# One expert-mixture kernel, four edits: state decay on GpSimd, rows turned in three stages, first expert's W2 split ahead of its gate, first expert's rows scaled by ScalarE

## The chip, the cores and the metric

The kernel runs on one core of one Trainium2 chip. The metric is the device time of one execution in microseconds, the median of several. The engines are named as in the profile: PE is TensorE, PEld its weight loads, DVE is VectorE, ACT is ScalarE, POOL is GpSimd, SP is SyncE, which here only issues transfers.

## The reference

A linear attention with a decay for each head, in blocks, feeds a mixture of eight experts of which each token takes two.

```python
for b in range(nb):                      # q, k, v: 4 x 8 x 768 x 64, blocks of 64
    intra = einsum('bhic,bhjc->bhij', qb, kb) * Dmask[None]
    intra = einsum('bhij,bhjd->bhid', intra, vb)
    inter = einsum('bhid,bhde->bhie', qb * lam_pow[None], kv_state)
    out[:, :, sl] = intra + inter
    kv_state = lam_block * kv_state + einsum('bhsd,bhse->bhde', kb * rev_pow[None], vb)
x = out as 3072 x 512
noisy_logits = x @ w_gate + log1p(exp(x @ w_noise)) * noise
top2, top2_w = the two largest of 8 and their softmax
for e in range(8):                       # w1: 512 x 1024, w2: 1024 x 512
    out[mask] += top2_w[mask] * (relu(x[mask] @ w1[e]) @ w2[e])
```

## The kernel before

The instructions of every engine are issued in the order in which the program text emits them; nothing is reordered. Each engine works through its own queue, and an instruction that waits holds up everything behind it on that engine. There is therefore no planner of costs, only a hand-written order and a small one for the routing: `jobs` is a list of generators (the gate, the routing, the building of key blocks), and `advance(n)` emits steps of them on DVE until an amount of estimated time is used up. Where an `advance` stands decides where in DVE's queue those steps lie.

**Attention.** Twelve steps `u`, each of two chunks `a` of 128 tokens of one batch; three steps make a batch. A step turns K and Q on PE (`trans_k` L344, `trans_q` L360), forms the state's increment (`kv` L435, from `KD`, which POOL scales in `kdecay`, L376), the products inside the chunk (`scores` L388, masked by DVE at L391; `intra`, L400) and the products with the state (`inter`, L400, which read the decayed queries `qTs` and the states `SA`). Before, DVE makes `qTs` from PSUM (L367; for step 1 at L724), and `state` (L439) makes the next state by four multiply-adds for each chunk (L447), or a copy where a batch begins (L444). `KD` has one buffer, so `kdecay` of the next step waits until PE has read the last one in `kv`. `logits`, `gate`, `weights` and `route` (L498 to L640) choose experts for a third of the tokens at a time; their work tiles lie in one tile called `arena`. `pool_keys` (L659) and `keys` (L648) build one-hot blocks, on POOL and on DVE, from which PE makes the lists of rows (`enlist`, L684).

**Experts.** Weights and rows are split into two half-precision parts each (hi by ACT, lo by DVE), and every product is made of three matmuls. For every expert a first product (`gemm1`, L995, eight groups `f` of twelve matmuls for each of two or three parts of its tiles) is followed by a second (`gemm2`, L1040, or L1051 for a short last tile, over tiles of 128 tokens). `evac1` (L1001 on ACT, L1005 on DVE) takes every group out of PSUM: ACT writes hi, then DVE writes the rest lo. `pS` has four banks.

From the third expert on, rows are gathered in pieces and turned by DVE itself: `turn_rows` transposes a tile (L935) and ACT then copies it to half precision (L937) in the same call; `split_rows` makes lo (L947) and gives the buffers to the next gathers. Four tiles are turned during the `gemm2` of the expert before, the others while the first part of `gemm1` runs, at `f` even; `parts` puts the later tiles first, so that the part of four tiles comes second, and its first group needs the last turned tile.

**The first expert** (e = 0) has three parts, of two, two and three tiles, since its rows are gathered while routing still goes on. In part 0 the gate of the last third of the tokens is advanced on DVE between the `split_w(2, 0, j)` of W2 and the evacuations. In `half_lists`, called inside `gemm2` of tile 0, DVE reads the second lists (L699) and POOL gathers two tiles (L919), which `trans_rows` (L974 on PE, L976 on ACT, L977 on DVE) turns inside `gemm2` of tile 1. Results go to `PV` (L1046 on DVE) and are scattered by POOL.

Of the kernel before, what the change touches and what calls it, by code (L numbers as in the profile page):

```python
# [31 lines left out]
C = 128  # L32
# [101 lines left out]
def kernel(  # L134
# [215 lines left out]
    def trans_q(u, banks=()):  # L350

        scaled = not banks
        banks = iter(banks)
        qT[u] = aw.tile([128, HP, 2 * C], FT, name="qT", bufs=1)
        qTs[u] = aw.tile([128, HP, 2 * C], FT, name="qTs")
        for a in range(2):
            nm = next(banks, None)
            p = psum.tile([128, HP, C], FT, name=nm) if nm else bank()
            for hp in range(HP):
                nc.tensor.transpose(p[:, hp, :], QT[u][:, a, 2 * hp:2 * hp + 2, :], identf)  # L360
            cs = slice(a * C, (a + 1) * C)
            if u:
                nc.scalar.activation(qT[u][:, :, cs], p, AF.Copy)
            else:
                nc.vector.tensor_copy(qT[u][:, :, cs], p)
            if scaled and (u % NW or a):
                nc.vector.tensor_mul(qTs[u][:, :, cs], p, QS)  # L367
# [71 lines left out]
    def state(u):  # L439

        for a, p in enumerate(KV[u]):
            sn = SA[u + a, 1 - a] = next(states)
            if (u, a) not in SA:
                nc.vector.tensor_copy(sn, p[:, :, :D])  # L444
                continue
            for hp in range(HP):
                nc.vector.scalar_tensor_tensor(sn[:, hp, :], SA[u, a][:, hp, :], QS[:, hp, C - 1:C], p[:, hp, :D],  # L447
                                               op0=MULT, op1=ADD)
# [272 lines left out]
    state(0)  # L721
# [13 lines left out]
    state(1)  # L735
# [38 lines left out]
    WR = [rp.tile([128, NT], FT, name=f"wr{i}") for i in range(2)]  # L774
    W8 = [rp.tile([128, NT, E - 1], FT, name=f"w8{i}") for i in range(2)]
# [154 lines left out]
    def turn_rows(e, t):  # L930
# [6 lines left out]
        nc.scalar.activation(xt(0, slice(t * TS, t * TS + size(e, t))), raw, AF.Copy, scale=xsc[:, NG - 1:])  # L937
        turned.append((e, t, raw))

    def split_rows():  # L940

        if not turned:
            return
        e, t, raw = turned.pop(0)
# [84 lines left out]
    def gemm2(e, t, then={}):  # L1029
# [6 lines left out]
        if n == TS:  # L1036
# [5 lines left out]
            if e:  # L1042
                nc.vector.scalar_tensor_tensor(o, p, w, pv, op0=MULT, op1=ADD)  # L1043
                scatter_out(e, t, o)
            else:
                nc.vector.tensor_scalar(o, p, w, winv0[:n, part_of(t):part_of(t) + 1], op0=MULT, op1=MULT)  # L1046
# [9 lines left out]
        else:  # L1056
            nc.vector.tensor_scalar(w, w, winv0[:n, part_of(t):part_of(t) + 1], None, op0=MULT)
# [37 lines left out]
    for t in range(NST):  # L1095
# [6 lines left out]
        elif u < NST:  # L1102
            kv(u)
            state(u)
            kdecay(t + 2)
# [4 lines left out]
            trans_q(u)  # L1110
        if t in SQUARES:
# [76 lines left out]
    units = {1: [(1, c, 1, PV[c - 4].bitcast(BF)) for c in range(4, GB[2] - GB[1])], 2: []}  # L1188
    for unit in units[1][:POOLED]:
        pool_keys(*unit)  # L1190
    jobs.extend((build(units[1][POOLED:]), routing(NG - 1), build(units[2])))
    for f in range(2):
        evac1(0, 0, PARTS0[0], f, head[f])
    advance(1.0)
# [21 lines left out]
    def half_lists():  # L1216
        while not built:
            advance(0.01)
# [11 lines left out]
    for i, (t0, n) in enumerate(parts(0)):  # L1230
        for f in range(FB):
# [10 lines left out]
            if i == 0:  # L1242
                if f in (2, 4, 6, 7):
                    split_w(2, 0, (2, 4, 6, 7).index(f))
                else:
                    advance(FILL1)
# [16 lines left out]
        unscale(winv0[:, i:i + 1], 0, None)  # L1263
        if i == 2:
# [87 lines left out]
    for e in range(1, E):  # L1352
# [6 lines left out]
        for i, (t0, n) in enumerate(parts(e)):  # L1359
            for f in range(FB):  # L1360
# [3 lines left out]
                if e > 1 and i == 0 and f % 2 == 0:  # L1364
                    split_rows()
                    if nxt:
                        turn_rows(e, nxt.pop(0))
# [18 lines left out]
        split_rows()  # L1386
        assert not turned
        row_weights(e)
        nxt = tile_order(e + 1) if e + 1 < E else []
        for t in range(tiles(e)):  # L1390
# [3 lines left out]
            if e + 1 < E:  # L1394
# [5 lines left out]
                split_rows()  # L1400
                if t < EARLY:
                    turn_rows(e + 1, nxt.pop(0))
    with tc.For_i(0, n_over) as it:
# [79 lines left out]
```

## Time and profile before

| what | value |
|---|---|
| median of 3 runs | 698.88 us (695.11 to 699.32) |
| the profiled execution | 703.04 us, its span 701.2 us |
| busy PE, DVE, POOL, ACT | 669.4, 414.6, 371.3, 306.3 us |
| mean granted TensorE clock of the span | 0.988 |

The profile is one execution of its own, and its time lies 4.16 us above the median of the runs. The span runs from the first to the last instruction; 1.84 us lie around it. Attention fills the first 146 us, the first expert reaches to 231 us, and the other seven take the rest. Busy time is an average over these; which wait counts is read from the stage.

### The profile page before, as it was taken

The page shows a single profiled execution, that of the slowest core. Times are in us where ns is not written, and L with a number is a line of the kernel's source. Part 1 is how long each engine was busy: PE and PEld are TensorE (multiplying, and loading weights), DVE is VectorE, ACT ScalarE, POOL GpSimd, SP SyncE. Part 2 cuts the span into 40 slices and gives each one's busy share as a digit, 9 for nine tenths or more (in the row PEclk, how much of TensorE's full clock was granted, in tenths as well). Part 3 has the DMA queues.
Part 4 walks back from the last instruction along what each step waited for, and adds up shares of the span by engine and source line. Part 5 has one row for each costly group of instructions (what it writes and reads, how often), then busy time and mean ns, then how long its engine had stood idle before and what let it go on. Part 6 is the DMA issues. An engine that isn't in the chain of part 4 may idle for free.

```text
span 701.2 us, 15983 instructions
## 1 busy us (share of the span) xinstructions
PE 669.4 (95%) x6073; PEld 401.7 (57%) x6073; DVE 414.6 (59%) x1058; ACT 306.3 (44%) x528; POOL 371.3 (53%) x524
## 2 busy tenths in 40 slices
PE   8899899998999999999998999899999999999994
PEld 6788788884765464464445445544554474456441
DVE  4744878988746755664655465556656554565510
ACT  2257567772228453326433633363344436433300
POOL 4512162374154585668767846784677578531221
PEclk9999999999999999999999999999999999999997
DMA  9899888474574562525551545164427434411110
GB/s 200 221 260 235 222 233 229 150 266 156 132 230 150 156 193 84 172 59 157 173 175 43 170 143 174 45 197 131 147 71 210 145 101 145 144 46 39 58 52 33
DMA packets 94193, 104.32 MB, mean 149 GB/s; under 512 B 41235, under 2 KB 66845, under 8 KB 94113
## 3 DMA queue, kind: packets, MB, share of 16 engines
q1 hardware_dynamic: 79456, 65.73, 33.4%
q0 software_dynamic: 13552, 37.00, 16.4%
q8 instruction: 49, 0.80, 0.5%
q10 hardware_dynamic: 1104, 0.53, 0.4%
q14 instruction: 32, 0.25, 0.1%
HBM read 78.28 MB, written 26.12 MB: 149 GB/s over the span
## 4 chain that ended last, share of the span: by engine, by line
PE 66%; DVE 13%; issue 8%; DMA 4%; POOL 4%; ACT 2%; ACTq 0%; POOLq 0%; DVEq 0%
PE pS L995 26%; PE pKV L1040 13%; PE pO L1040 13%; PE pO L400 2%; DVE ht L1005 2%; PE pS L388 2%; PE pS L344 2%; DMA pv<-out_dram,rec 1%; POOL out_dram L1066 1%; DVE at L391 1%; PE pS L435 1%; PE pS L466 1%; PE pS L360 1%; ACT xth L937 1%; POOL xg L908 1%
## 5 line engine op out<-in xcount | busy, mean ns | idle before, releaser
L1040 PEld LDWEIGHTS <-ht 128*128 128x128 f16 x1152 | 112.2, 98 | 135.7 <-issue 3.1
L995 PE MATMUL pS<-xtl,w1h 128*128 128x512 f16 (+3 forms) x544 | 175.8, 323 | 4.7 <-DVE xtl L947 4.7
L995 PE MATMUL pS<-xth,w1h 128*128 128x512 f16 (+3 forms) x544 | 175.7, 323 | 3.7 <-ACT xth L937 2.0
L908 POOL DMA_INDIRECT xg<-x_tok,recq x147 | 153.6, 1045 | 45.9 <-issue 41.0
L995 PE MATMUL pS<-xth,w1l 128*128 128x512 f16 (+3 forms) x544 | 175.7, 323 | 0.0
L995 PEld LDWEIGHTS <-w1h 128*128 128x128 f16 x1088 | 105.5, 98 | 72.3 <-issue 8.0
L1005 DVE SCALAR_TENSOR_TENSOR ht<-pS,ht 128x256 f16<-128x256 f32 (+3 forms) x176 | 75.6, 455 | 103.5 <-ACT ht L1001 102.9
L1001 ACT ACTIVATE ht<-pS 128x512 f16<-128x512 f32 (+3 forms) x136 | 63.1, 479 | 147.6 <-PE pS L995 144.7
L1040 PE MATMUL pKV<-w2h,ht 128*128 128x512 f16 x384 | 119.1, 381 | 0.0
L1040 PE MATMUL pO<-w2h,ht 128*128 128x512 f16 x384 | 118.1, 379 | 0.0
L1066 POOL DMA_INDIRECT out_dram<-ot,rec x46 | 61.5, 1337 | 102.7 <-DVE ot L1043 73.6
L937 ACT ACTIVATE xth<-turned,xsc 128x512 f16<-128x512 f32 (+1 forms) x39 | 27.2, 697 | 120.5 <-DVE turned L935 120.5
L995 PEld LDWEIGHTS <-w1l 128*128 128x128 f16 x544 | 53.3, 98 | 38.7 <-issue 6.1
L1040 PE MATMUL pO<-w2l,ht 128*128 128x512 f16 x192 | 72.8, 379 | 1.1 <-DVE w2l L873 1.1
L1040 PE MATMUL pKV<-w2l,ht 128*128 128x512 f16 x192 | 73.3, 382 | 0.0
L855 ACT ACTIVATE junk<-wst 128x1024 bf16<-128x1024 f32 x64 | 67.0, 1046 | 0.0
L376 POOL TENSOR_TENSOR kd<-kt,Mk 128x512 f32<-128x512 f32 x24 | 24.8, 1051 | 79.0 <-PE pR L435 55.5
L1024 POOL DMA_INDIRECT pv<-out_dram,rec x46 | 52.6, 1144 | 13.4 <-issue 13.4
L873 DVE SCALAR_TENSOR_TENSOR w2l<-wst,wsc,w2h 128x1024 f16<-128x1024 f32 x32 | 41.1, 1284 | 9.1 <-ACT w2h L872 8.6
L1043 DVE SCALAR_TENSOR_TENSOR ot<-pO,wr,pv 128x512 f32<-128x512 f32 x21 | 15.8, 751 | 49.7 <-PE pO L1040 49.1
L391 DVE TENSOR_TENSOR at<-pS,Mk 128x512 f32<-128x512 f32 x48 | 29.9, 682 | 22.9 <-PE pS L388 19.8
L873 DVE SCALAR_TENSOR_TENSOR w1l<-wst,wsc,w1h 128x1024 f16<-128x1024 f32 x32 | 40.6, 1275 | 0.0
(261 smaller groups left out, 896.2 us busy)
## 6 DMA issues: line engine op xcount, KB each, us to landing
wst<-in_moe_w_dram SPq DMA_DIRECT2D x36, 512.0 KB, 3.6
wst<-in_moe_w_dram SPq DMA_DIRECT2D x96, 128.0 KB, 2.8
x_tok<-xc SPq DMA_DIRECT2D x24, 272.0 KB, 5.0
kt<-in_k_dram SPq DMA_DIRECT2D x12, 512.0 KB, 4.5
qt<-in_q_dram SPq DMA_DIRECT2D x24, 256.0 KB, 5.7
vt<-in_v_dram SPq DMA_DIRECT2D x12, 512.0 KB, 6.0
out_dram<-zero SPq DMA_DIRECT2D x24, 256.0 KB, 3.8
xg<-x_tok,recq POOLq DMA_INDIRECT x147, 2.8
```

The costliest lines, as they stand in the source:

```text
L376: nc.gpsimd.tensor_mul(kd[:, :, s], kt[:, :, s], mask(s, slice(0, HP), slice(C - 1, C)).to_broadcast([128, HP, 2, D]))
L391: nc.vector.tensor_mul(at[:, s], ps[s], mask(s, slice(2 * r, 2 * r + 2), slice(0, C)))
L855: nc.scalar.activation(junk, WS[which, e, j], AF.Square, accum_out=wsq[:, which - 1, j:j + 1])
L873: nc.vector.scalar_tensor_tensor(lo[:, r], st[:, r], s, hi[:, r], op0=MULT, op1=SUB)
L908: nc.gpsimd.indirect_dma_start(out=XG[t][:, g * QW:(g + 1) * QW], out_offset=None, in_=x_tok.rearrange("t (q w) -> (t q) w", w=QW), in_off ...
L937: nc.scalar.activation(xt(0, slice(t * TS, t * TS + size(e, t))), raw, AF.Copy, scale=xsc[:, NG - 1:])
L995: nc.tensor.matmul(p, W1[a][d][:, fs], xt(b, cs)[:, d], start=(d == 0 and i == 0), stop=(d == DB - 1 and i == 2))
L1001: nc.scalar.activation(ht(e, 0, f, cs), p, AF.Relu)
L1005: nc.vector.scalar_tensor_tensor(ht(e, 1, f, c), p[:, r], 0.0, ht(e, 0, f, c), op0=OP.max, op1=SUB)
L1024: nc.gpsimd.indirect_dma_start(out=PV[t][:size(e, t), :], out_offset=None, in_=out, in_offset=bass.IndirectOffsetOnAxis(ap=REC[e, t], axis=0),
L1040: nc.tensor.matmul(p, ht(e, a, f, cs), W2[b][f // 2][:, f % 2, :], start=(i == 0), stop=(i == len(terms) - 1))
L1066: st = nc.gpsimd.indirect_dma_start(out=out, out_offset=bass.IndirectOffsetOnAxis(ap=REC[e, t], axis=0), in_=o, in_offset=None, bounds_che ...
```

## The change

Four things change. Nothing of the mathematics does.

1. **Attention.** The decayed queries come from POOL, out of the half of `qT` that ACT has written, not from DVE out of PSUM. The state is made in two parts: POOL multiplies the last state by its decay into a tile `sd` (`decay`), and DVE adds the increment from PSUM in one instruction for each chunk. `decay` of the next chunk is emitted directly behind `state`. In the loop the second chunk's `state` and `kdecay` now stand behind `trans_q`, and the gathers of the first expert stand between the two halves.
2. **Turned rows.** The copy by ACT has a function of its own, `copy_rows`, called one group `f` (or one tile of `gemm2`) after the turn. `split_rows` takes what has been copied.
3. **First expert, part 0.** `advance(1.0)` and the advances at `f` = 3 and 5 go. Only the one key block that DVE builds is emitted at `f` = 3. The gate begins inside `half_lists`. Of the four key blocks of the last third, POOL builds one (`late`), and DVE three.
4. **First expert's output.** ACT copies the sums with the row's weight as scale; the scale of the part is multiplied into the weights once for each part on DVE.

```diff
@@ trans_q, state
-                nc.vector.tensor_mul(qTs[u][:, :, cs], p, QS)
+                nc.gpsimd.tensor_mul(qTs[u][:, :, cs], qT[u][:, :, cs], QS)
...
-    def state(u):
-        for a, p in enumerate(KV[u]):
+    def decay(u, a):
+        if (u, a) in SA:
+            SD[u, a] = aw.tile([128, HP, D], FT, name="sd")
+            nc.gpsimd.tensor_mul(SD[u, a], SA[u, a], QS[:, :, C - 1:C].to_broadcast([128, HP, D]))
+    def state(u, a):
+        if a < len(KV[u]):
+            p = KV[u][a]
             sn = SA[u + a, 1 - a] = next(states)
-            if (u, a) not in SA:
+            if (u, a) in SD:
+                nc.vector.tensor_add(sn, SD[u, a], p[:, :, :D])
+            else:
                 nc.vector.tensor_copy(sn, p[:, :, :D])
-                continue
-            for hp in range(HP):
-                nc.vector.scalar_tensor_tensor(sn[:, hp, :], SA[u, a][:, hp, :], QS[:, hp, C - 1:C], p[:, hp, :D],
-                                               op0=MULT, op1=ADD)
+            decay(u + a, 1 - a)
@@ start and loop of attention
-    state(0)
+    state(0, 0)
+    state(0, 1)
...
-    state(1)
+    state(1, 0)
+    state(1, 1)
...
+    nc.gpsimd.memset(WR[0], 0.0)
...
             kv(u)
-            state(u)
-            kdecay(t + 2)
+            state(u, 0)
             if REC and not got:
                 ...
             trans_q(u)
+            state(u, 1)
+            kdecay(t + 2)
@@ turned rows
-        nc.scalar.activation(xt(0, slice(t * TS, t * TS + size(e, t))), raw, AF.Copy, scale=xsc[:, NG - 1:])
         turned.append((e, t, raw))
+    copied = []
+    def copy_rows():
+        if turned:
+            e, t, raw = turned.pop(0)
+            nc.scalar.activation(xt(0, slice(t * TS, t * TS + size(e, t))), raw, AF.Copy, scale=xsc[:, NG - 1:])
+            copied.append((e, t, raw))
     def split_rows():
-        if not turned:
+        if not copied:
             return
-        e, t, raw = turned.pop(0)
+        e, t, raw = copied.pop(0)
...
-                if e > 1 and i == 0 and f % 2 == 0:
-                    split_rows()
-                    if nxt:
-                        turn_rows(e, nxt.pop(0))
+                if e > 1 and i == 0:
+                    copy_rows()
+                    if f % 2 == 0:
+                        split_rows()
+                        if nxt:
+                            turn_rows(e, nxt.pop(0))
...
-                split_rows()
+                copy_rows()
                 if t < EARLY:
                     turn_rows(e + 1, nxt.pop(0))
+                if t:
+                    split_rows()
@@ first expert
+    def late():
+        pool_keys(*units[2][-1])
+        yield 0.01
+        yield from build(units[2][:-1])
-    jobs.extend((build(units[1][POOLED:]), routing(NG - 1), build(units[2])))
+    jobs.extend((build(units[1][POOLED:]), routing(NG - 1), late()))
...
-    advance(1.0)
...
     def half_lists():
-        while not built:
-            advance(0.01)
...
                     split_w(2, 0, (2, 4, 6, 7).index(f))
-                else:
-                    advance(FILL1)
+                while f == 3 and not built:
+                    advance(0.01)
...
+        nc.vector.tensor_scalar(WR[0][:, t0:t0 + n], WR[0][:, t0:t0 + n], winv0[:, i:i + 1], None, op0=MULT)
...
-                nc.vector.tensor_scalar(o, p, w, winv0[:n, part_of(t):part_of(t) + 1], op0=MULT, op1=MULT)
+                nc.scalar.activation(o, p, AF.Copy, scale=w)
...
-            nc.vector.tensor_scalar(w, w, winv0[:n, part_of(t):part_of(t) + 1], None, op0=MULT)
             nc.vector.tensor_scalar(o, p[:n, :], w, None, op0=MULT)
```

## Rows read from the trace of the kernel before

**Rows 1.** Stretches: busy PE, PEld, DVE, ACT, POOL (x instructions), granted clock, DMA.

```profile
51.07:61.53 10.46, 10.46 (x258) 9.00 (x258) 5.31 (x15) 7.26 (x14) 2.06 (x2) 1.00 1.04 190
165.00:201.00 36.00, 32.73 (x226) 20.71 (x225) 23.43 (x106) 7.70 (x16) 13.69 (x36) 0.95 0.48 133
```

**Rows 2.** Waits of PE between 299 and 570 us: total, times, longest.

```profile
PE pS L995 <- DVE xtl L947: 4.7, 3, 1.6
PE pS L995 <- ACT xth L937: 2.0, 2, 1.0
PE pS L995 <- DVE ht L1005: 0.8, 1, 0.8
```

**Rows 3.** Timeline of PE at step 11; brackets: idle before, what ended it.

```profile
128.88 1.85 PE L344 MATMUL pS<-identf,kt 128*128 128x128 f32 x12 [0.75 <-DVE at L391]
```

**Rows 4.** Timeline of ACT at the start of expert 3: start, duration, instruction.

```profile
374.17 0.72 ACT L937 ACTIVATE xth<-turned,xsc 128x512 f16<-128x512 f32 x1 [2.82 <-DVE turned L935]
374.80 0.69 ACT L1001 ACTIVATE ht<-pS 128x288 f16<-128x288 f32 x2
```

**Rows 5.** Timeline of DVE there.

```profile
372.46 0.74 DVE L947 SCALAR_TENSOR_TENSOR xtl<-turned,xsc,xth 128x512 f16<-128x512 f32 x1
...
375.23 0.95 DVE L1005 SCALAR_TENSOR_TENSOR ht<-pS,ht 128x256 f16<-128x256 f32 x4 [1.09 <-ACT ht L1001]
...
379.73 0.74 DVE L947 SCALAR_TENSOR_TENSOR xtl<-turned,xsc,xth 128x512 f16<-128x512 f32 x1
```

**Rows 6.** Chain that ended last, second part of gemm1 in experts 2 and 3.

```profile
312.52 20.66 PE pS L995 x95
...
380.52 22.09 PE pS L995 x95
```

**Rows 7.** One tile's instructions: arena (busy PE, DVE, POOL); pv (PE, PEld, DVE, POOL).

```profile
152.00:170.10 18.10, 0.00 (x0) 8.23 (x53) 0.46 (x2) 1.00 0.68 249
...
148.90:159.80 10.90, 0.00 (x0) 0.00 (x0) 1.04 (x4) 10.12 (x18) 1.00 0.94 336
```

**Rows 8.** Timelines of ACT and DVE in the first expert.

```profile
159.95 1.14 ACT L872 ACTIVATE w2h<-wst,wsc 128x1024 f16<-128x1024 f32 x1
...
164.10 1.28 DVE L873 SCALAR_TENSOR_TENSOR w2l<-wst,wsc,w2h 128x1024 f16<-128x1024 f32 x1
...
166.15 0.17 DVE L699 TENSOR_SCALAR recs<-idfTrue 128x2 int32<-128x2 f32 x1
...
174.01 0.75 DVE L977 SCALAR_TENSOR_TENSOR xtl<-pS,xsc,xth 128x512 f16<-128x512 f32 x1 [1.22 <-ACT xth L976]
```

**Rows 9.** Timeline of PE in the first expert.

```profile
163.90 0.38 PE L1040 MATMUL pO<-w2l,ht 128*128 128x512 f16 x1 [1.07 <-DVE w2l L873]
...
170.56 0.66 PE L974 MATMUL pS<-identf,xg 128*128 128x128 f32 x4 [1.31 <-DMA xg<-x_tok,recs]
172.16 1.09 PE L974 MATMUL pS<-identf,xg 128*128 128x128 f32 x4 [0.95 <-DMA xg<-x_tok,recs]
...
177.18 0.27 PE L995 MATMUL pS<-xth,w1h 128*128 128x256 f16 x1
```

**Rows 10.** Timeline of POOL at the start of attention.

```profile
22.02 1.05 POOL L770 MEMSET xg<- 128x544 f32 x2
...
23.64 0.24 POOL L1093 MEMSET xc<- 128x64 f32 x2
27.84 2.06 POOL L376 TENSOR_TENSOR kd<-kt,Mk 128x512 f32<-128x512 f32 x2 [3.96 <-PE pR L435]
```

**Rows 11.** Chain that ended last: PE's state increment of step 2.

```profile
32.00 1.08 PE pS L435 x32
```

**Rows 12.** Timelines of DVE and POOL: one conversion, and one multiplication at two places.

```profile
120.53 1.02 DVE L699 TENSOR_SCALAR recs<-idfTrue 128x2 int32<-128x2 f32 x1
...
103.01 0.85 POOL L587 TENSOR_TENSOR arena<-arena 128x64 f32<-128x64 f32 x1
...
181.57 0.32 POOL L587 TENSOR_TENSOR arena<-arena 128x64 f32<-128x64 f32 x1
```

More of the change, by code (lines that the diff above doesn't have):

```diff
@@ L437, in kv @@
         KV[u] = ps
-    def state(u):
-        for a, p in enumerate(KV[u]):
+    SD = {}
+    def decay(u, a):
[5 more added lines that the diff above has]
+            p = KV[u][a]
             sn = SA[u + a, 1 - a] = next(states)
-            if (u, a) not in SA:
+            if (u, a) in SD:
+                nc.vector.tensor_add(sn, SD[u, a], p[:, :, :D])
+            else:
                 nc.vector.tensor_copy(sn, p[:, :, :D])
-                continue
-            for hp in range(HP):
-                nc.vector.scalar_tensor_tensor(sn[:, hp, :], SA[u, a][:, hp, :], QS[:, hp, C - 1:C], p[:, hp, :D],
-                                               op0=MULT, op1=ADD)
+            decay(u + a, 1 - a)
     def products(u):
@@ L1385 @@
             prepare(e + 2)
-        split_rows()
-        assert not turned
+        assert not turned and not copied
         row_weights(e)
@@ L1399 @@
                     square_w(2, e + 1, t - 1)
-                split_rows()
+                copy_rows()
                 if t < EARLY:
                     turn_rows(e + 1, nxt.pop(0))
+                if t:
+                    split_rows()
     with tc.For_i(0, n_over) as it:
```

## The prediction

> **What bounds the kernel now.** I read the busy time by stretches first, then the waits of PE, then the timelines around each wait. In a plain attention step PE is busy for the whole step, 10.46 of 10.46 us [rows 1]: work taken from DVE there buys nothing. So the reader should look for the places where PE stands still, since only these can be won. In the experts three kinds of wait make up PE's idle time between 299 and 570 us: 4.7, 2.0 and 0.8 us [rows 2], 7.5 us in all. They lie where the second part of gemm1 starts, in experts 2 to 5. In the first expert the stretch from 165 to 201 us has 32.73 of 36.00 us busy, at a mean clock of 0.95 [rows 1]. In attention one wait for DVE, 0.75 us, stands at step 11 [rows 3].
>
> **Part 1: turned rows.** At the start of expert 3, DVE and ACT take turns. ACT's copy stands in its queue ahead of two evacuations, and it waits 2.82 us for DVE's turn [rows 4]; DVE's evacuations wait 1.09 us for ACT's behind that copy, and the next turn stands behind them [rows 5]. The first split of a turned tile starts at 372.46, the third at 379.73 [rows 5], so a loop takes 3.64 us for two groups of gemm1. PE's wait ends with that third split.
>
> With the copy one group later, ACT writes the evacuation of the odd group before it waits. The chain of a loop is then turn, copy, one evacuation on ACT and one on DVE, split, turn. One pair of DVE's evacuations leaves it, because it runs beside the copy; four instructions take 0.95 us [rows 5], so a pair is 0.45 to 0.48 and the loop 3.64 - 0.45 = 3.2 us. In the first loop all that is queued behind the first turn is ready, so it loses the whole idle time of 1.09 us [rows 5] and wins back 0.1 us of handing over: the first split stands near 371.5 in place of 372.46. The third is then at 371.5 + 2 x 3.2 = 377.9 in place of 379.73: 1.8 us less. Expert 4 has the same three waits and gives the same. Expert 2 starts behind one partial sum of a short tile, not three, so that DVE is less late: two loops, 0.9 us, and some 0.3 us of the first, 1.2 us. Expert 5 has two turns in gemm1 and waits only for a PSUM bank, 0.8 us [rows 2]; that goes. Sum: 1.2 + 1.8 + 1.8 + 0.8 = 5.6 us. What is late next is the same split, by under 1 us. Bounds: 3 us if half of it comes, 7.5 us if all waits go.
>
> Behind its waits the clock fell in expert 3: the same 95 matmuls took 22.09 us there and 20.66 us in expert 2 [rows 6]. That is 1.4 us. Expert 4 has the same waits without it, so I take half, 0.7 us (0 to 1.4).
>
> **Part 2: first expert.** Now DVE's instructions on the gate are mixed with the splits of W2. The gate's tiles (the arena) keep DVE busy for 8.23 us between 152 and 170 us [rows 7], about half of it ahead of the second lists. These are written at 166.15, behind a last split that starts at 164.10, though ACT's half for it was done at 159.95 + 1.14 = 161.1 [rows 8]. Without the gate that split starts at 161.1, 3.0 us sooner; a new multiplication of the weights takes some 0.2 us, so the lists stand at 163.4, 2.8 us sooner. PE's wait of 1.07 us for that split ends, so PE is ready for the gathered rows at 170.56 - 1.31 - 1.07 = 168.2 [rows 9]. The rows come 170.56 - 166.3 = 4.3 us behind the lists for the first tile, and 1.6 us later for the second [rows 9]: at 167.8 and 169.4. From there PE needs about 3 us for the transposes and the second tile's twelve products (5.0 us from 172.16 to 177.18 before [rows 9], part of it at a lower clock): until 172.5.
>
> What is late next is the gate itself. It begins at 163.5 and takes 8.2 us, and about 1 us for the gaps between its instructions and the maximum of the squares: until 172.7. Two splits of gathered rows stand behind it on DVE, 0.75 us each, the second of which began at 174.01 before [rows 8]: now at 173.5, done at 174.3. The second part's gemm1, which began at 177.18 [rows 9], then begins at about 174.3: 2.9 us sooner. From there DVE works off the route as before, with one key block less. POOL's three blocks of one chunk took 10.12 us [rows 7], so the block of two chunks takes 2 x 3.4 = 6.7 us behind the weights, which moves to about 178.5: it ends near 185.2, when PE needs it. I keep 2.9 us (1.3 us if that block comes 1.6 us late; 4.4 us if the gate isn't late either).
>
> ACT now waits in order for the sums of tiles 4 and 5, with halves of W1 for expert 1 queued behind them; DVE's halves, and with them PE's first products of expert 1, wait for these. Loads are there in time, and the slack is about as long as the delay; I take 0.3 us lost (0 to 0.72, one copy by ACT [rows 4]).
>
> **Part 3: attention.** DVE loses two multiplications and six of eight short instructions in a step, some 2 us. In plain steps this is worth nothing. At step 11 it removes the 0.75 us for which the transposes wait [rows 3]: 0.8 us won (0 to 1.1). The second addition now waits about 0.7 us for POOL's decay, with steps of the gate behind it on DVE; the 2 us cover that.
>
> The start costs. POOL's memsets ran from 22.02 to 23.88; kdecay of step 2 started at 27.84, as soon as PE had read the last KD, and took 2.06 us [rows 10]; PE came to use it at 32.00 [rows 11]. The order now puts four decays and these memsets ahead of it. The third decay waits for DVE's state(1, 0), which can't start before PE ends kv(1) at 27.8. From there: an addition (0.45, as an evacuation of 256 columns), a decay (0.55, half of one kdecay instruction), the second addition (0.45), the second decay (0.55), 0.3 us of handing over and 1.9 us of memsets: kdecay starts at 32.0 and ends at 34.1. PE waits; the loss is 34.2 - 32.0 = 2.2 us. PE is full in the steps behind, so it stays. Bounds: 0.6 us (a later stall of PE takes some back) to 4 us (the clock falls behind this wait, as in expert 3).
>
> **The sum.** -5.6 - 0.7 - 2.9 + 0.3 - 0.8 + 2.2 = -7.5 us. Against the profiled execution, 703.04 us, this gives 695.5 us. The runs' median lies 4.16 us below that execution, and I leave that difference as it is: 698.88 - 7.5 = 691.4 us.
>
> **A rule that speaks against the change.** DVE's conversion of two columns took 1.02 us where POOL multiplied beside it [rows 12] and 0.17 us where it did not [rows 8]. In turn a POOL multiplication of 64 columns took 0.85 us beside DVE's key building, and 0.32 us elsewhere [rows 12]. The Trainium skill, GPSIMD Engine Reference, section "8. Key points", says that GpSimd shares its SBUF interfaces with VectorE, with contention where a DVE instruction runs in a two-port mode or has two SBUF inputs. By that rule, the trace agrees, more POOL work slows both engines; what it would do here is rival A.
>
> **The rivals.** (A) POOL becomes the bound of attention and the kernel slower. A step's POOL work is then 2.1 us for kd [rows 1], 2.1 for the queries and 1.1 for the decays, 5.3 us of 10.46. So it decides from a stretch of 2.0. With the 2.6 of the 64-column multiplication [rows 12] a step needs 13.8 us, 3.3 too many; in the six steps in which DVE's gate and key building run that is +20 us in place of -0.8: 712 us. Against it: much of DVE's work there is short or reads PSUM.
>
> (B) It comes near to no change. If the loop keeps its old length, since turn and copy stay in one chain, the experts give only the sooner first splits, 0.3 + 0.9 + 0.9, and the bank wait, 0.8: 2.9 us. If POOL's key block holds the first expert, that gives 1.3 us. With +2.2, +0.3 and -0.8 the sum is -2.5 us, 696.4 us.
>
> (C) All waits of the experts go (7.5 us), the clock stays up (1.4 us), the first expert gives 4.4 us and half of the loss at the start is taken back: -7.5 - 1.4 - 4.4 + 1.1 - 0.8 + 0.3 = -12.7 us, 686.2 us.
>
> **Chances.** About 1% is what a measurement of this kernel can tell from no change, 7 us, so the bound lies at 691.9. Forecast (688 to 694.5): 0.50, of which 0.30 lies below the bound. C (below 688): 0.22. B (694.5 to 702): 0.20. A, or any other loss: 0.08. So faster 0.52, same 0.40, slower 0.08. The range leaves out A, the end of B and the end of C: 685.5 to 698.5.
>
> **What would show it.** The trace of the changed kernel should show, in ACT's timeline of experts 2 to 4, the copy behind the odd group's evacuation, and splits 3.2 us apart on DVE; PE's wait ahead of the second part under 1 us; the second lists about 2.8 us sooner behind the start of the first expert; kdecay of step 2 behind the memsets and PE waiting there for POOL. Wrong would be: no wait at kv(2), a gate that ends much later than 9 us behind the lists, or POOL's instructions stretched to twice their length in steps 5 to 10.

## The result, and the profile after

The changed kernel takes 706.53 us (median of 6 runs, 705.0 to 709.19) where the kernel before takes 699.14 us (6 runs beside it, 695.11 to 699.78): a ratio of 1.0117, 95% interval 1.0087 to 1.0146. It is slower by 7.4 us by the medians (6.1 to 10.2 by the interval); 691.4 us were forecast. The span of the profiled execution is 705.4 us against 701.2 us. Edit 1 is the prediction's part 3, edit 2 its part 1, edits 3 and 4 its part 2. Parts 1 and 2 did what they should, attention did not.

**Experts.** PE's waits between 299 and 570 us, then the chain of waits of expert 3's second part:

```profile
PE pS L1014 <- DVE xtl L966: 2.5, 3, 1.0
```

```profile
389.18 20.66 PE pS L1014 x95
```

Of the 7.5 us in three kinds of wait [rows 2], 2.5 us in one kind are left, and the 95 matmuls take 20.66 us, not 22.09 [rows 6]. DVE's splits and ACT at the start of expert 3 (start, duration, instruction):

```profile
381.96 0.74 DVE L966 SCALAR_TENSOR_TENSOR xtl<-turned,xsc,xth 128x512 f16<-128x512 f32 x1
...
385.17 0.75 DVE L966 SCALAR_TENSOR_TENSOR xtl<-turned,xsc,xth 128x512 f16<-128x512 f32 x1
...
388.39 0.74 DVE L966 SCALAR_TENSOR_TENSOR xtl<-turned,xsc,xth 128x512 f16<-128x512 f32 x1
```

```profile
382.18 0.41 ACT L1020 ACTIVATE ht<-pS 128x288 f16<-128x288 f32 x1 [0.69 <-PE pS L1014]
383.68 0.72 ACT L956 ACTIVATE xth<-turned,xsc 128x512 f16<-128x512 f32 x1 [1.09 <-DVE turned L946]
```

The splits stand 3.21 and 3.22 us apart (before, 3.64 [rows 5]), and an evacuation now runs ahead of the copy that waits for DVE.

**First expert.** DVE, and then PE where the second part begins:

```profile
178.25 0.17 DVE L707 TENSOR_SCALAR recs<-idfTrue 128x2 int32<-128x2 f32 x1
...
188.14 0.75 DVE L996 SCALAR_TENSOR_TENSOR xtl<-pS,xsc,xth 128x512 f16<-128x512 f32 x1
188.80 0.14 DVE L1001 COPY wr<-xg 128x1 f32<-128x1 f32 x1
188.86 0.74 DVE L996 SCALAR_TENSOR_TENSOR xtl<-pS,xsc,xth 128x512 f16<-128x512 f32 x1
```

```profile
188.38 0.27 PE L1014 MATMUL pS<-xth,w1h 128*128 128x256 f16 x1
189.66 0.27 PE L1014 MATMUL pS<-xtl,w1h 128*128 128x256 f16 x1 [1.00 <-DVE wr L1001]
```

The first expert's first product stands at 160.54 us in PE's timeline (145.74 before). Counted from there, the second lists are written 2.7 us sooner (17.71 against 20.41 [rows 8]), and the second part has all its rows at 29.1 in place of 31.4 us [rows 9]: 2.3 us sooner.

**The start of attention.** POOL, then PE:

```profile
21.86 0.62 POOL L445 TENSOR_TENSOR sd<-S,QS 128x256 f32<-128x256 f32 x1
23.01 1.00 POOL L445 TENSOR_TENSOR sd<-S,QS 128x256 f32<-128x256 f32 x1 [0.54 <-DVE S L453]
28.25 0.62 POOL L445 TENSOR_TENSOR sd<-S,QS 128x256 f32<-128x256 f32 x1 [4.24 <-DVE S L453]
29.41 0.62 POOL L445 TENSOR_TENSOR sd<-S,QS 128x256 f32<-128x256 f32 x1 [0.53 <-DVE S L453]
29.96 1.04 POOL L780 MEMSET xg<- 128x544 f32 x2
...
31.80 2.06 POOL L376 TENSOR_TENSOR kd<-kt,Mk 128x512 f32<-128x512 f32 x2
```

```profile
28.32 0.29 PE L400 MATMUL pKV<-qTs,S 64*64 64x128 f32 x1 [1.78 <-DVE S L453]
32.91 0.47 PE L435 MATMUL pS<-vt,kd 64*64 64x64 f32 x2 [1.81 <-POOL kd L376]
33.91 1.97 PE L435 MATMUL pS<-vt,kd 64*64 64x64 f32 x30 [0.54 <-POOL kd L376]
```

The last line is the new thing: 30 matmuls take 1.97 us where 32 took 1.08 [rows 11]. The granted clock says why (stretch: busy PE, PEld, DVE, ACT, POOL, clock, DMA):

```profile
33.00:41.00 8.00, 7.46 (x120) 6.74 (x120) 0.42 (x1) 1.19 (x2) 4.84 (x5) 0.57 0.53 130
```

The same 8 us stand at 1.00 before, and in e5 and e13 below: behind the waits PE ran near its lower level, 1.2 of 2.4 GHz.

**Step 10.** DVE, POOL, and PE where step 11 begins:

```profile
130.17 7.17 DVE L109 SCALAR_TENSOR_TENSOR arena<-arena 128x64 f32<-128x64 f32 x6
...
137.60 1.52 DVE L542 SCALAR_TENSOR_TENSOR arena<-arena 128x64 f32<-128x64 f32 x6
139.04 2.48 DVE L391 TENSOR_TENSOR at<-pS,Mk 128x512 f32<-128x512 f32 x4
```

```profile
130.84 1.03 POOL L930 DMA_INDIRECT xg<-x_tok,recs  x1 [0.30 <-PE pS L474]
131.90 2.51 POOL L367 TENSOR_TENSOR qTs<-qT,QS 128x512 f32<-128x512 f32 x2
134.35 0.64 POOL L445 TENSOR_TENSOR sd<-S,QS 128x256 f32<-128x256 f32 x1
134.93 2.06 POOL L376 TENSOR_TENSOR kd<-kt,Mk 128x512 f32<-128x512 f32 x2
```

```profile
139.78 2.82 PE L344 MATMUL pS<-identf,kt 128*128 128x128 f32 x12 [4.11 <-DVE at L391]
```

```profile
139.80:152.00 12.20, 12.20 (x164) 10.67 (x168) 8.71 (x40) 5.88 (x11) 5.45 (x14) 0.62 0.01 2
```

Six short instructions of the gate take 7.17 us; six of the same kind take 1.52 us two lines below. With 0.26 us for each of the others, one of them takes 7.17 - 5 x 0.26 = 5.9 us (5.87 in the timeline, from 131.21): it ends only where POOL's products, which follow each other without a gap, end (134.93 + 2.06 = 137.0). It begins 0.7 us ahead of the first of them, while the second gather (L930) still runs. DVE's masks (L391) stand behind it in the queue, and PE waits 4.11 us for them, where it waited 0.75 us [rows 3]. Then the clock is 0.62 for 12 us.

**Where the time went.** The start of each stage on PE (its first transpose of K, or its first product, in PE's timeline):

| stage, us | before | after |
|---|---|---|
| to step 3 | 40.78 | 45.49 |
| steps 3 to 9 | 76.92 | 78.44 |
| step 10 | 11.18 | 15.85 |
| step 11 to the first expert | 16.86 | 20.76 |
| first expert | 85.20 | 81.96 |
| other experts to the end | 470.30 | 462.86 |

The first row varies from one execution to the next: over the twelve kernels of this text whose start is that of before it lies between 37.64 and 42.78, mean 39.4, and over the five with the changed start between 44.39 and 46.22, mean 45.4. So the start costs 6.0 us.

The row of step 11 varies too. Behind the same wait of 4.11 or 4.10 us that stretch takes 18.00 us in e2, 17.74 in e5 and 18.27 in e13 (runs told below), at a granted clock of 0.86, 0.89 and 0.84 over its first 12.2 us, where the changed kernel has 20.76 us at 0.62. So the slow clock cost 0.9 to 3.9 us there. In e2 part of the slow stretch lay inside the wait, where PE lost nothing by it (granted clock of step 10: 0.89, against 0.97 in the changed kernel). What sets when it begins and ends is not shown.

### The profile page after: what moved, and what is told of

Same layout as the page of the kernel before. It is cut to its first block, busy times and chain, and to the rows that moved or that the text cites. A ratio compares the mean times of both kernels' runs of the same rounds, so it can differ in the third digit from the quotient of the medians.

```text
span 705.4 us, 15969 instructions
## 1 busy us (share of the span) xinstructions
PE 669.4 (95%) x6073; PEld 404.3 (57%) x6073; DVE 409.9 (58%) x983; ACT 312.6 (44%) x534; POOL 411.5 (58%) x574
## 4 chain that ended last, share of the span: by engine, by line
PE 60%; DVE 6%; issue 5%; ACT 1%; POOL 1%; DMA 1%; POOLq 0%; DVEq 0%; ACTq 0%
PE pS L1014 29%; PE pKV L1059 15%; PE pO L1059 15%; POOL out_dram L1084 1%; PE pO L1070 1%; DVE xtl L966 1%; DVE ot L1078 1%; ACT xth L956 1%; DVE turned L946 1%; PE pS L993 1%; DVE ht L1024 1%; PE pKV L1070 1%; DMA pv<-out_dram,rec 0%; DMA xg<-x_tok,recq 0%; ACT ht L1020 0%
## 5 line engine op out<-in xcount | busy, mean ns | idle before, releaser
L919 POOL DMA_INDIRECT xg<-x_tok,recq x147 | 155.7, 1059 | 45.9 <-issue 40.4
L1020 ACT ACTIVATE ht<-pS 128x512 f16<-128x512 f32 (+3 forms) x136 | 65.2, 481 | 170.0 <-PE pS L1014 159.6
L1043 POOL DMA_INDIRECT pv<-out_dram,rec x46 | 48.9, 1064 | 13.5 <-issue 13.5
L883 ACT ACTIVATE w1h<-wst,wsc 128x1024 f16<-128x1024 f32 x32 | 36.5, 1142 | 30.2 <-DVE wsc L497 30.2
L391 DVE TENSOR_TENSOR at<-pS,Mk 128x512 f32<-128x512 f32 x48 | 29.9, 683 | 31.5 <-PE pS L388 26.1
L884 DVE SCALAR_TENSOR_TENSOR w2l<-wst,wsc,w2h 128x1024 f16<-128x1024 f32 x32 | 41.2, 1287 | 10.2 <-ACT w2h L883 9.7
L445 POOL TENSOR_TENSOR sd<-S,QS 128x256 f32<-128x256 f32 x20 | 12.8, 642 | 56.8 <-DVE S L453 39.9
```

Of the source, the lines that this page charges most:

```text
L391: nc.vector.tensor_mul(at[:, s], ps[s], mask(s, slice(2 * r, 2 * r + 2), slice(0, C)))
L883: nc.scalar.activation(hi[:, r], st[:, r], AF.Copy, scale=s)
L884: nc.vector.scalar_tensor_tensor(lo[:, r], st[:, r], s, hi[:, r], op0=MULT, op1=SUB)
L919: nc.gpsimd.indirect_dma_start(out=XG[t][:, g * QW:(g + 1) * QW], out_offset=None, in_=x_tok.rearrange("t (q w) -> (t q) w", w=QW), in_off ...
L1020: nc.scalar.activation(ht(e, 0, f, cs), p, AF.Relu)
L1043: nc.gpsimd.indirect_dma_start(out=PV[t][:size(e, t), :], out_offset=None, in_=out, in_offset=bass.IndirectOffsetOnAxis(ap=REC[e, t], axis=0),
```

## The experiments

The theory that I began with: the gains of the two later parts are real and add up; attention loses at its start (POOL's queue, then the clock) and at step 10, where POOL's multiplications of SBUF tensors lock out DVE's instructions on SBUF. The rivals: the long DVE instruction waits for data; the order on POOL's queue (gathers, memsets) does it alone; or the gains come only from the later start. Ratios are to the kernel before, which ran beside each kernel at 699.6 to 699.7 us.

### e1, e15: the attention part undone

```diff
-                nc.gpsimd.tensor_mul(qTs[u][:, :, cs], qT[u][:, :, cs], QS)
+                nc.vector.tensor_mul(qTs[u][:, :, cs], p, QS)
...
-            state(u, 0)
+            state(u)
+            kdecay(t + 2)
...
-            state(u, 1)
-            kdecay(t + 2)
```

> The changed kernel with its attention part undone; the three other edits stay. If the loss comes from the attention part (theory), the experts keep the 6.4 us and the first expert the 2.8 us that the two traces show, so 699.1 - 9.2 = 690 us (688 to 692), and the first product of the first expert stands within 1 us of the kernel before. If the loss hangs on the other parts, or the gains hang on the shift that attention gives them (rival), the time stays at 697 us or above.

> The changed kernel with its attention part undone, once more, beside the next run. By stages of the traces the experts give 7.1 and the first expert 2.6 us: 699.6 - 9.7 = 689.9 us, 2.6 us below the next run. Rival (the first expert's edits give nothing beside the turned rows): both within 1 us.

Measured: 690.89 us, ratio 0.9867 (0.984 to 0.9893), and again 689.33 us, 0.9848 (0.9818 to 0.9879). All of the loss is attention's. This is the fastest kernel of the study, and faster than both. PE's wait at step 11 is 0.75 us in e15, as before the change.

### e2: the attention part alone

> The kernel before with the attention part alone. Theory: the first expert starts some 14.8 us later and nothing gives it back, 699.1 + 14 = 713 us (711 to 716), with one instruction of DVE held for 5 to 6 us at step 10. Rival (the parts disturb each other, attention alone costs what was forecast, 1.4 us): 700 to 703 us and no held instruction.

Measured: 713.88 us, ratio 1.0198 (1.0171 to 1.0225). PE waits 4.11 us at step 11 here too, and one instruction of DVE takes 5.85 us.

### e9, e16: the turned rows alone; e10: the first expert alone

> The kernel before with the three stages of the turned rows alone. Theory (the experts' gain stands by itself): the waits ahead of the second part of gemm1 fall as in the changed kernel, from 1.57, 2.56, 2.56 and 0.78 us to 0.57, 0.94, 0.97 and 0 us, and the clock stays up in expert 3: 699.1 - 5.0 - 1.4 = 692.7 us (691.5 to 694.5). Rival (part of it came from the later start, which gave the loads of the experts more time): 695 us or more.

> The kernel before with the three stages of the turned rows alone, once more. By stages of the traces 699.6 - 7.1 = 692.5 us; 690.8 was measured first. Rival as above: 690 to 691 us, within 1 us of the run before this one.

> The kernel before with the edits of the first expert alone (W2's splits ahead of the gate, a key block on POOL, rows scaled by ACT). Theory: 2.8 us as between the two traces, 696.3 us (695 to 697.5). Rival (the shorter first expert in the changed kernel came from its slower attention, behind which loads and lists were further ahead): 698.5 us or more.

Measured: 690.81 us, 0.9871 (0.9848 to 0.9893), and again 693.38 us, 0.989 (0.9858 to 0.9922), for the rows; 696.17 us, 0.9951 (0.9927 to 0.9976), for the first expert. The first pair of medians, 690.81 alone and 690.89 with the first expert's edits (e1), looked as if the latter gave nothing beside the rows. Run side by side, e15 is 4.1 us below e16. By stages, the other experts take 463.36 (e9), 463.19 (e1) and 470.08 us (e10), and the first expert 82.65 us in e10 and e1: 7.1 and 2.6 us, and they add up. (Between e16 and e15 the first expert gives 3.5 us.) e9's time lies 0.7 us below the expected range. e10 holds edits 3 and 4 together; what each gives alone was not run.

### e5: the start as before

```diff
             else:
                 nc.vector.tensor_copy(sn, p[:, :, :D])
-            decay(u + a, 1 - a)
+            if u > 1:
+                decay(u + a, 1 - a)
...
             kdecay(2)
+            decay(2, 0)
```

Where there is no `sd`, `state` uses the multiply-adds of before.

> The changed kernel with its start as before: the states of the first two steps by DVE's multiply-adds, and the one decay that is left there (for step 2) behind kdecay of step 2. Theory (the start's loss is POOL's queue: two decays that wait for DVE and 1.9 us of memsets ahead of kdecay): kdecay starts near 28 us in place of 31.8, step 3 begins near 40.8 in place of 45.5, and the rest keeps its loss: 706.5 - 4.7 = 701.8 us (700 to 703). Rival (step 3 is late for another reason, such as the loads): 705 to 707 us.

Measured: 700.11 us, ratio 0.9988 (0.996 to 1.0016): 6.4 us below the changed kernel. kdecay of step 2 starts at 27.64, step 3 at 40.35 us, and PE's 4.11 us wait at step 11 stays.

### e13: the memsets behind kdecay

> The changed kernel with the memsets of the first rows, the weights and the spare columns (1.4 us of POOL's 1.9) behind kdecay of step 2 in place of ahead of it; the decays stay. If POOL's queue as a whole makes the start's loss: kdecay starts near 30.5 us in place of 31.8, PE's wait for it falls from 1.8 to about 0.5 us, and some of the slow clock behind it goes: 702.5 to 705.3 us. If the two decays that wait for DVE make it alone: 706 to 707 us. If the slow clock hangs on that last wait: 702.5 us or less.

Measured: 704.27 us, ratio 1.0061 (1.0042 to 1.0081). POOL, and the stretch in which the clock had fallen:

```profile
30.52 2.06 POOL L376 TENSOR_TENSOR kd<-kt,Mk 128x512 f32<-128x512 f32 x2
```

```profile
33.00:41.00 8.00, 8.00 (x210) 6.85 (x205) 2.65 (x5) 4.46 (x9) 6.02 (x12) 1.00 0.86 228
```

kdecay starts 1.3 us sooner, PE's wait for it falls to 0.29 us, the clock stays at 1.00, and step 3 begins at 41.48 us, 2.9 us or more ahead of the kernels with the changed start. So in this execution 1.3 us of POOL's queue cost more than its length, by way of the clock. The kernel as a whole gains 2.3 us: in this profile steps 3 to 9 take 80.51 us in place of 78.44, with the clock at 0.61 in the first 4.4 us of step 9.

### e3: the queries by DVE; e4: the state by DVE

e3:

```diff
-                nc.gpsimd.tensor_mul(qTs[u][:, :, cs], qT[u][:, :, cs], QS)
+                nc.vector.tensor_mul(qTs[u][:, :, cs], p, QS)
```

e4 takes `decay` away, and `state(u, a)` makes its half by the multiply-adds of before.

> The changed kernel with the decayed queries made by DVE from PSUM again; POOL keeps the decays. Theory (DVE is held for as long as POOL multiplies without a gap): POOL's run at step 10 falls from five instructions (6.3 us from the gate's start of the hold to its end) to a decay and two of kdecay, 2.7 us, so the hold is at most 2.7 us; PE's 4.1 us wait and the 3.9 us of slow clock behind it go, the start stays: about 706.5 - 7 = 699.5 us (698 to 702). Rival (the decays and the order of state are at fault): 704 to 707 us.

> The changed kernel with the state made by DVE's multiply-adds again (in halves, at the places of the change), no decay on POOL; POOL keeps the decayed queries. Theory: the loss of the start goes (4.7 us less 0.1 us), since nothing stands ahead of the memsets; POOL's run at step 10 is still two multiplications and two of kdecay, 4.6 us, so DVE is held there for 4 to 5 us and most of that loss stays: 701 to 704 us. Rival (the decays are at fault in both places): 693 to 696 us.

Measured: e3 700.98 us, 1.0019 (0.9997 to 1.0041); e4 697.39 us, 0.9962 (0.9938 to 0.9987). DVE and POOL at step 10, in e3 and then in e4:

```profile
127.70 3.23 DVE L109 SCALAR_TENSOR_TENSOR arena<-arena 128x64 f32<-128x64 f32 x2
...
128.20 0.63 POOL L445 TENSOR_TENSOR sd<-S,QS 128x256 f32<-128x256 f32 x1
128.78 2.06 POOL L376 TENSOR_TENSOR kd<-kt,Mk 128x512 f32<-128x512 f32 x2
```

```profile
121.04 6.05 DVE L109 SCALAR_TENSOR_TENSOR arena<-arena 128x64 f32<-128x64 f32 x4
...
121.70 2.52 POOL L367 TENSOR_TENSOR qTs<-qT,QS 128x512 f32<-128x512 f32 x2
124.17 2.05 POOL L376 TENSOR_TENSOR kd<-kt,Mk 128x512 f32<-128x512 f32 x2
```

The hold follows POOL's run in both, whatever it multiplies (in e3, 0.3 us of the 3.23 lie ahead of the run, at the end of the gather).

e3's time lies in its range, but not for the reason forecast, and that is luck: the slow clock behind step 10 was to go, and the stretch from step 11 on still takes 19.79 us (20.76 in the changed kernel, 16.86 before). Step 10 gives 3.0 us and that stretch 1.0; the rest comes from the start (1.1) and from steps 3 to 9 (2.1).

e4's time is 3.6 us below the theory's range. Its hold is as expected (PE waits 4.22 us at step 11), but the start had been counted as 4.7 and not 6.0 us, and steps 3 to 9, step 10 and the stretch behind it are each some 1 us shorter than in the changed kernel.

### e14: the start as before and the queries by DVE

> The changed kernel with both: the start as before, and the decayed queries by DVE from PSUM; POOL keeps the decays of the other steps. If the attention loss is a start and a step 10 that add up: against the kernel with the attention part undone, 690.9 us, only the 2.7 us hold and the slow clock behind it stay, 4.6 us by the traces: 695.5 us (694 to 697). If the decays cost something in the steps between too: 698 us or more.

Measured: 695.18 us, ratio 0.9933 (0.9914 to 0.9952). The two losses can be taken away one by one; PE waits 2.48 us at step 11 for the decay and kdecay that are left on POOL, as in e3 (2.45 us).

### e6: the gathers behind POOL's multiplications

```diff
-            if REC and not got:
-                ...
             trans_q(u)
             state(u, 1)
             kdecay(t + 2)
+            if REC and not got:
+                ...
```

> The changed kernel with the two gathers of step 10 behind the whole POOL work of that step in place of ahead of it. Theory (what decides the hold is that POOL has all its work ready behind the gathers and does it without a gap): the multiplications come as they become ready, each DVE instruction is held for one or two of them (up to 2.6 us, as at step 7), PE's wait of 4.1 us and the slow clock behind it go for the most part: 706.5 - 6 = 700.5 us (698 to 703). Rival (POOL's amount of work in the step decides): 705 to 707 us.

Measured: 705.69 us, ratio 1.0077 (1.0048 to 1.0105): the rival. DVE:

```profile
129.94 0.91 DVE L121 TENSOR_SCALAR arena<-arena 128x64 f32<-128x64 f32 x1
130.88 1.23 DVE L109 SCALAR_TENSOR_TENSOR arena<-arena 128x64 f32<-128x64 f32 x1
132.03 0.62 DVE L124 TENSOR_SCALAR arena<-arena 128x64 int32<-128x64 f32 x1
132.58 1.09 DVE L126 TENSOR_SCALAR arena<-arena 128x64 f32<-128x64 f32 x1
133.71 1.34 DVE L109 SCALAR_TENSOR_TENSOR arena<-arena 128x64 f32<-128x64 f32 x2
```

POOL beside it:

```profile
129.52 2.51 POOL L367 TENSOR_TENSOR qTs<-qT,QS 128x512 f32<-128x512 f32 x2
131.98 0.63 POOL L445 TENSOR_TENSOR sd<-S,QS 128x256 f32<-128x256 f32 x1
132.56 2.06 POOL L376 TENSOR_TENSOR kd<-kt,Mk 128x512 f32<-128x512 f32 x2
```

No instruction is held for long, as I had forecast, but each waits for one of POOL's. DVE loses 3.9 us in place of 5.7, PE waits 3.44 us in place of 4.11, and the kernel's time hardly moves (0.8 us). So it matters little how the hold is cut up; my idea that the gathers made it costly falls.

The gathers do decide the form of the hold. POOL's five products follow each other without a gap here too, and DVE still gets one instruction through behind each. In the eighteen traces one instruction is held over a whole run of three to five products eight times (the changed kernel, e2 to e5, e12 to e14), each time where the run stands directly behind a gather. In the 119 other cases where a short instruction of DVE (under 0.4 us) was held and POOL's next product followed without a gap, it ended within 0.25 us of the end of one product. Behind a gather DVE is also held early, from 0.5 to 0.7 us ahead of POOL's first product in the timeline; in the kernel before, where nothing stands behind the gathers on POOL, DVE's instruction at that place (0.62 us before the second gather ends) takes its usual 0.19 us. Why a gather ahead makes this difference is not shown.

### e7, e12, e8: work added on POOL in the kernel before

```diff
                     gather_rows(0, j, GB[1] * C)
                 got.append(t)
+                dm = aw.tile([128, HP, C], FT, name="dm", bufs=1)
+                for _ in range(5):
+                    nc.gpsimd.tensor_mul(dm, QS, QS)
```

e12 writes two such tiles in turn; e8 has `tensor_scalar(dm, QS, 1.5, ...)` in place of the product. Nobody reads the result.

> The kernel before with five multiplications of 128x512 added on POOL behind the gathers of step 10; their result goes to a tile of their own that nobody reads. Theory (a DVE instruction with two SBUF inputs gets through only where POOL's run of multiplications has a gap): one of the gate's instructions takes about 5.2 us, DVE's mask at L391 is some 4.5 us late, and PE's wait at step 11 grows from 0.75 to about 5 us: 699.1 + 4.5 and up to 4 for the clock, 704 to 708 us. Rival (the long instruction in the changed kernel waited for data or for a semaphore): no long instruction, 699 to 700 us.

> The kernel before with the five added multiplications again, now writing two tiles in turn, so that POOL waits for no semaphore between them. With one tile there was a gap of 0.08 us behind each, and DVE got one instruction through in each. Theory: without gaps one instruction of DVE takes the whole 5.2 us, and the loss of time is the same as with gaps (704 to 708 us), because DVE's lost time is POOL's busy time either way. Rival (gaps decide how much is lost): 709 us or more, or under 703 us.

> As the run before, but each of the five POOL instructions multiplies by a constant, so that it has one tensor as input. If any POOL instruction on SBUF holds DVE: one instruction of the gate as long as the run of the five, and a loss by that length. If only POOL instructions with two tensor inputs do: no instruction of the gate over 1.2 us, 699 to 700 us.

Measured: e7 706.50 us, 1.0076 (1.0047 to 1.0106); e12 707.01 us, 1.0097 (1.0064 to 1.0129); e8 702.55 us, 1.0035 (1.0005 to 1.0064). DVE and POOL in e7, then in e12:

```profile
122.72 1.76 DVE L124 TENSOR_SCALAR arena<-arena 128x64 int32<-128x64 f32 x1
...
124.61 4.62 DVE L109 SCALAR_TENSOR_TENSOR arena<-arena 128x64 f32<-128x64 f32 x5
...
123.37 5.52 POOL L1112 TENSOR_TENSOR dm<-QS 128x512 f32<-128x512 f32 x5
```

```profile
123.26 5.72 DVE L124 TENSOR_SCALAR arena<-arena 128x64 int32<-128x64 f32 x1
...
123.91 5.02 POOL L1112 TENSOR_TENSOR dm<-QS 128x512 f32<-128x512 f32 x5
```

These products have nothing to do with attention's data, and DVE is held all the same: the rival "it waits for data" falls. In e7 POOL waits for its own last write between two products (5.52 us for five, 0.3 us of it gaps), and DVE gets one instruction through each time. In e12 there is no gap, and one instruction takes 5.72 us. Both kernels lose the same time. With one tensor input (e8) POOL needs 1.49 us for each. One instruction of DVE beside each of the first three loses 0.3 to 0.4 us, since it ends only 0.7 us behind the start of POOL's, and one more loses 0.4 us at the end of the gather; the others take their usual time while POOL goes on. PE waits 2.15 us at step 11, 1.4 us more than before. The result lies between the two expectations, and why this form lets DVE go before its end stays open.

### e11: the gate moved away from POOL's run

```diff
-            advance(FILLS)
+            advance(FILLS if t != 9 else 0)
...
-        advance(FILL - (SPLIT if t in SPLITS else 0))
+        advance(FILL - (SPLIT if t in SPLITS else 0) + (FILLS if t == 9 else 0))
```

> The changed kernel with one advance of the gate moved: in the step before the last of attention with a state, the 3.4 us of gate that stood beside POOL's multiplications follow at the end of the step, behind the masks; no work is removed on either engine. Theory (the loss at step 10 is DVE's gate instructions held beside POOL, with the masks behind them): no instruction of the gate over 1.2 us, PE's 4.1 us wait and the slow clock behind it go, 706.5 - 8 = 698.5 us (697 to 701). Rival (POOL's longer work or its gathers delay PE directly, by qTs): 704 to 707 us.

Measured: 702.31 us, ratio 1.0038 (1.0018 to 1.0058), between the two. DVE and POOL at step 10, then the granted clock in step 11:

```profile
132.06 2.48 DVE L391 TENSOR_TENSOR at<-pS,Mk 128x512 f32<-128x512 f32 x4 [3.25 <-PE pS L388]
134.46 2.89 DVE L884 SCALAR_TENSOR_TENSOR w1l<-wst,wsc,w1h 128x1024 f16<-128x1024 f32 x1
...
131.16 2.51 POOL L367 TENSOR_TENSOR qTs<-qT,QS 128x512 f32<-128x512 f32 x2
133.62 0.63 POOL L445 TENSOR_TENSOR sd<-S,QS 128x256 f32<-128x256 f32 x1
134.21 2.05 POOL L376 TENSOR_TENSOR kd<-kt,Mk 128x512 f32<-128x512 f32 x2
```

```profile
145.00:154.80 9.80, 8.79 (x146) 6.98 (x147) 9.35 (x31) 5.23 (x10) 6.52 (x22) 0.83 0.58 213
```

The masks, which read PSUM and one SBUF tensor, run beside POOL's products at their usual 2.48 us; the split behind them, with two SBUF tensors, takes 2.89 in place of 1.28 us. Step 10 shrinks from 15.85 to 11.58 us. But the gate now stands ahead of DVE's state of step 11, POOL's decay and queries behind that, and PE waits 1.19 us for the queries (L367); the clock falls once more, and step 11 to the first expert takes 20.02 us. Of the 8 us forecast 4.2 came; the rest is lost one step later.

## Why the prediction was wrong

**What decides at step 10.** Lost on DVE: the time of its gate instructions beside POOL's run, less what they take elsewhere (0.19 to 0.26 us each).

| kernel | POOL's run, us | lost on DVE, us | PE's wait at step 11, us |
|---|---|---|---|
| after | 5.1, five products | 7.17 - 1.52 = 5.7 | 4.11 |
| e6 | 5.1, five | 5.19 - 1.3 = 3.9 | 3.44 |
| e4 | 4.5, four | 6.05 - 1.0 = 5.0 | 4.22 |
| e3 | 2.6, three | 3.23 - 0.5 = 2.7 | 2.45 |
| e7 | 5.5, five with gaps | 6.38 - 1.5 = 4.9 | 5.64 |
| e12 | 5.0, five | 5.72 - 0.2 = 5.5 | 6.26 |

This is shown by adding the work (e7, e12), by taking it away (e3, e1) and by moving DVE's side of it (e11). In this table DVE loses 0.8 to 1.1 times as long as POOL multiplies.

**Part 1, turned rows: right.** The loop was to be 3.2 us and is 3.21 and 3.22; the third split of expert 3 was to come 1.8 us sooner, and counted from the first product of expert 3 (365.63 before, 376.06 after, in PE's timeline) it comes 388.39 - 376.06 = 12.33 us behind it in place of 379.73 - 365.63 = 14.10. With the clock, 6.3 us were forecast; by stages it is 7.1, and 6.3 and 8.8 us by the runs of e16 and e9. Of the waits 5.0 us went (5.6 forecast), and the clock gave the full 1.4 us in expert 3 (0.7 counted).

**Part 2, first expert: right.** The lists are 2.7 us sooner (2.8 forecast), the gate ends 9.8 us behind them (9.2), and the stage is 2.6 to 3.5 us shorter (2.9 less 0.3). The second part has its rows 2.3 us sooner, where 2.9 were forecast. The loss of 0.3 us by ACT's order is too small to be seen.

**Part 3, attention: wrong in two terms, and a third put at nothing.** Net +1.4 us was forecast. The stages give 6.0 at the start, 2.0 in steps 3 to 9 (78.0 to 78.5 us in five kernels with this part and 80.5 in a sixth, e13; 76.4 in nine without), 4.7 in step 10 and 3.9 behind it: 16.6 us. The runs give 713.88 - 699.62 = 14.3 us (e2) and 706.53 - 689.33 = 17.2 us (against e15). The two differ by about as much as the stretch behind step 10, 18.00 us in e2 and 20.76 in the changed kernel.

The first failing step is "0.8 us won (0 to 1.1)" with "the 2 us cover that". It counted the instructions that leave DVE, and nothing for what POOL's new ones do to those that stay. The sign turned: -0.8 became +5.6 to +8.6 us at step 10 and behind it, by how much of the slow clock fell behind the wait. Rival A named the contention but priced it the wrong way round: POOL's products keep their length at step 10 (1.28 us for one of the queries, 0.64 for a decay; the longest of the queries' is 1.73, beside DVE's key blocks in step 8), and DVE's instructions stand still. So the measured time comes nearest to A's 712 us, but by another route. "Much of DVE's work there is short" is no protection, since an instruction of 0.23 us was held for all of POOL's run; "or reads PSUM" is one, as e11's masks show. The row that had it was there: a conversion of 0.17 us took 1.02 us beside kdecay [rows 12], which is one whole product of POOL (1.05 us), not a factor.

The Trainium skill, SBUF — State Buffer, section "🔬 SBUF: two separate sides", says that GpSimd and a DVE instruction with two SBUF inputs or in a two-port mode take the shared port pair by an exclusive lock for a whole instruction, and that the other is blocked. The traces agree for the products with two inputs where no gather stands ahead: in e6 each held instruction ends with one product. They differ from it in two places, and there the measurement decides: behind a gather DVE came in only at the end of the whole run (in e12 behind the fifth product), and in e8 it came in 0.7 us behind the start of an instruction of POOL that took 1.49 us.

The second failing step is the start, 2.2 us with bounds of 0.6 to 4. Its mechanism was right: kdecay at 32.0 (measured 31.80), PE's waits for it 1.81 + 0.54 us. Two things were left out: PE's products with the state wait 1.78 us in place of 0.38 us (at 28.09 us in PE's timeline of before), since the decay stands in the chain of the state, and the clock fell to 0.57 for the 8 us behind. Only the clock had been thought of, as a bound, and at too low a price; e13 shows that taking 1.3 us out of the queue keeps it up. That it is the length of these waits that decides over the clock was not tried apart from this.

The third is the term put at nothing, "in plain steps this is worth nothing": steps 3 to 9 lost 2.0 us. This was not taken apart. Without POOL's queries the stretch took 76.4 us in e3 and 78.4 in e14, without its decays 77.4 (e4), and the new order of the steps was never undone alone.

## What to carry to other kernels

Moving work from DVE to POOL is no relief where DVE has work on SBUF tensors at the same time: price each POOL product of two tensors at up to its full length taken from DVE, and ask which engine waits behind the instruction that is held. Give a wait on PE a second price for the clock, as a range and not as a multiple of the wait: here 0.9 to 3.9 us behind waits of 4.1 us, 2.9 to 3.0 behind 2.5 us (e3, e14), 0.9 behind 6.3 us (e12). When a bundle of edits turns out slower, undo it part by part: here two parts were worth 10 us and the third cost 14 to 17.

## What the runs showed of the hardware

- A DVE instruction of 0.2 us took 5.7 us beside five POOL products that stood directly behind a gather, without a gap between them (e12); with gaps of 0.08 us one instruction went through in each (e7). Where no gather stood ahead, one went through behind each product, gap or no gap (e6).
- It happened to DVE instructions with two SBUF inputs (L109) and with one (L124), not to those with a PSUM input (L391 at 0.62 us each for four, e11). Beside a gather with no product queued behind it DVE's instructions took their usual time; with one queued, the hold began up to 0.7 us ahead of that product.
- Behind PE's waits of 4.1 us at step 11 the slow clock cost 0.9 to 3.9 us in four traces (the changed kernel, e2, e5, e13).
- On POOL the product of a tensor of 512 columns with itself took 1.04 us, and that tensor by a constant 1.49 us (e7, e8).
- The start of attention varies by 5 us between profiled executions of kernels that have the same start.
